# Where the slot index products of a routing group stand: four of seven groups moved by one table

## The chip, the cores and the metric

The kernel runs on one core of a Trainium2 chip. The metric is the device time of one execution in microseconds (us); before the change it is 647.14 us, the median of three runs (646.2 to 647.47). PE is the matrix engine, DVE the vector engine, ACT the scalar engine, POOL the GpSimd engine and SP the engine that issues most DMAs. PSUM is the memory that PE writes its products to and from which DVE and ACT read them.

## The reference

Attention over 8 batches, 8 heads, 576 positions and 64 numbers a head, with a causal window of 128 and a bias that falls with distance; its output, as 4608 rows ("tokens") of 512 numbers, goes into a layer of 8 experts, each token to one.

```
mask = (rel >= 0) & (rel < window)
scores = np.where(mask, scores + bias[None], -1000000000.0)
attn = np.exp(scores - max); attn = attn / (sum + 1e-09)
x = attn @ v, as (4608, 512)
logits = x @ w_gate; expert_idx = argmax(logits)
for e in range(8):
    h = np.maximum(xe @ w1[e], 0.0); ye = h @ w2[e]
    out[mask] = gate_w[mask, None] * ye
```

The tokens of an expert are gathered, computed together in tiles of 128 and scattered back. So each token needs a slot: its rank among the tokens of its expert, and each slot needs the index of its token. Finding these is the routing.

## The kernel before, in words

**Two stages.** First comes attention with the routing worked in, then the experts (`moe_static`). Attention goes over 36 chunks of 128 tokens. Its order is written out by hand, step by step: `step(s)` is called for s = 0 to 151 and records, engine by engine, what is to be done; each engine then runs its instructions in just that order. A chunk `ch` begins at step 4·ch, and the table `LAGS` says at which later steps its parts come: scores on PE (L167 the bias, L176 query times key) at steps that leave remainder 0 and 2 modulo 4, masks and row maxima on DVE (L189, L192), exponentials on ACT (L198), transposes on PE (L211) with copies on ACT (L213) and masks on POOL (L221, L223), products with v on PE (L239) at remainder 3 and some at 0, and at remainder 1 the turning back of a chunk with its gate logits on PE (L249) and the division on DVE (L254, `x_sb`).

**The PSUM tile r_ps.** L249 writes into `r_ps`, a tile of 4 quarters of 256 fp32 numbers in each of 128 partitions; of each quarter it uses the columns 0 to 143 (`XW` is 144). There is one buffer: the next chunk's L249 gets it when all readers of the last are done. The routing borrows the unused columns: `spare(st, k, n)` is quarter k of the present `r_ps`, from column 144 on. Quarter 0 serves the rank products, quarter 1 the slot index products, quarter 2 a sum in `shift_late`.

**The routing.** The chunks form groups (`GROUPS`): 0 to 4, 5 to 9, 10 to 14, 15 to 20, 21 to 26, 27 to 29, 30 to 34, and 35 by itself. When the last chunk of a group is divided, `route` is made for it, a generator in five parts:

1. expert of each token, as ones and zeros `oh` (DVE, L473 to L486, ACT L480);
2. rank products: matmuls of a triangle of ones with `oh` into quarter 0 (PE, L490, L491, L494), their use on DVE (L496 `pick`, L504 `rank`), gates (L498, L560, L562, two or more small DMAs on SP, L565) and running counts (L501, L502);
3. position in a slot tile, `lp` (DVE, L515 to L522);
4. `rr`, token numbers sorted by expert and tile (DVE, L524 to L531);
5. slot index products: two bf16 matmuls a chunk of `lp` with `rr`, summed in quarter 1 (PE, L537), and their sum onto `base` (DVE, L539).

At the end of each step the loop over `st["stages"]` runs one part of every group whose turn it is, the older group first. A group that `PACE` does not list takes a part at every step with remainder 3, from the first one after its last chunk; a group that `PACE` lists takes its parts at the steps listed. So before the change the fifth parts of the first four groups came at steps 51, 71, 91 and 115, and the second parts of the groups from chunk 5, 10, 15 and 21 at steps 59, 79, 103 and 126. `lp` and `rr` come from a pool of two buffers (`RB`). `base` is read when all groups up to chunk 26 are in it, at step 135 (`early("g")`).

```
        for k in list(st["stages"]):
            if k[1] <= s and (s in PACE[k[2]] if k[2] in PACE else s % 4 == 3):
                k[1] = s + 1
                if next(k[0], k) is k:
                    st["stages"].remove(k)
```

**Waits.** The recording layer puts in the semaphore waits itself: an instruction that writes a tile waits for earlier readers of it, one that reads it for its writer.

Of the kernel before, what the change touches and what calls it, by code (L numbers as in the profile page):

```python
# [35 lines left out]
def attention(ctx, tc, st, qT, kT, v, iw, load_c2, chunk_done, chunks, begun):  # L36
# [295 lines left out]
    def step(s):  # L332
# [11 lines left out]
# [3 lines that stand above are left out]
# [57 lines left out]
LW = (0, 0, 0, 0)  # L404
FREE_T = 146
WU = (6, 0, 0, 1, 1, 0, 0, 0, 0, 0, 0, 1, 0)
PACE = {21: (122, 126, 130, 132, 135), 27: (135, 139, 143, 146, 148), 30: (149, 150)}
GROUPS = ((0, 5), (5, 5), (10, 5), (15, 6), (21, 6), (27, 3), (30, 5), (35, 1))
EARLY = 256
LATE = 27  # L410
# [783 lines left out]
def attn_moe_kernel(ctx, tc, qT, kT, v, c2, iw, w12, out):  # L1194
# [9 lines left out]
    with ExitStack() as actx:  # L1204
# [9 lines left out]
        def done(ch, subs, x_sb):  # L1214
# [14 lines left out]
            if g == G - 1:  # L1229
# [14 lines left out]
                else:  # L1244
                    r = route(tc, st, lg, c0, G, groups)
                    st["stages"].append([r, st["step"] + (c0 not in PACE), c0])

# [46 lines left out]
```

## Time and profile before

| | before |
|---|---|
| median of 3 runs | 647.14 us |
| the profiled execution | 646.91 us, span of its instructions 645.2 us |
| granted PE clock | 0.998 |
| PE busy | 632.1 us, 98% of the span |
| DVE busy | 390.9 us, 61% |
| ACT busy | 314.1 us, 49% |
| POOL busy | 299.2 us, 46% |

The 1.7 us between the span and the time of that execution lie outside the instructions. In the profile's lines each row of a timeline gives the start in us, the duration in us, the engine, the line of the kernel, the operation, the tile written and those read, how many instructions are merged into the row, and in brackets how long the engine stood idle before it and on whom it waited. PEld is the loading of PE's weights, which runs beside its matmuls. A row of waits gives the sum in us, the number of times and the longest.

### The profile page before, as it was taken

The page shows a single profiled execution, that of the slowest core. Times are in us where ns is not written, and L with a number is a line of the kernel's source. Part 1 is how long each engine was busy: PE and PEld are TensorE (multiplying, and loading weights), DVE is VectorE, ACT ScalarE, POOL GpSimd, SP SyncE. Part 2 cuts the span into 40 slices and gives each one's busy share as a digit, 9 for nine tenths or more (in the row PEclk, how much of TensorE's full clock was granted, in tenths as well). Part 3 has the DMA queues.
Part 4 walks back from the last instruction along what each step waited for, and adds up shares of the span by engine and source line. Part 5 has one row for each costly group of instructions (what it writes and reads, how often), then busy time and mean ns, then how long its engine had stood idle before and what let it go on. Part 6 is the DMA issues. An engine that isn't in the chain of part 4 may idle for free.

```text
span 645.2 us, 15063 instructions
## 1 busy us (share of the span) xinstructions
PE 632.1 (98%) x5681; PEld 540.2 (84%) x5681; DVE 390.9 (61%) x978; ACT 314.1 (49%) x947; POOL 299.2 (46%) x414
## 2 busy tenths in 40 slices
PE   8999999999998999999999999999999999999995
PEld 4888888888887988888988898898898888888884
DVE  6578888969898785545544654555455355346411
ACT  5878889888867324433333334334233333424311
POOL 5534657769446040166236707633660660561202
PEclk9999999999999999999999999999999999999999
DMA  9958998988734263372534325333442542534101
GB/s 312 301 153 216 220 260 237 217 258 240 193 69 103 54 196 98 130 273 75 186 128 151 108 78 183 113 94 139 142 122 83 165 122 87 185 107 143 65 0 62
DMA packets 57645, 97.90 MB, mean 152 GB/s; under 512 B 11669, under 2 KB 31765, under 8 KB 56674
## 3 DMA queue, kind: packets, MB, share of 16 engines
q1 hardware_dynamic: 49090, 76.89, 39.9%
q0 software_dynamic: 8336, 19.76, 10.6%
q8 instruction: 46, 0.75, 0.5%
q10 hardware_dynamic: 144, 0.26, 0.2%
q14 instruction: 29, 0.24, 0.1%
HBM read 77.91 MB, written 18.98 MB: 150 GB/s over the span
## 4 chain that ended last, share of the span: by engine, by line
PE 67%; ACT 0%; DVE 0%; issue 0%; POOLq 0%; POOL 0%; ACTq 0%
PE y_ps L907 32%; PE l_ps L711 30%; PE s_ps L711 2%; PE x_ps L672 1%; PE b_ps L239 1%; PE y_ps L867 1%; PE r_ps L249 0%; PE x_ps L867 0%; ACT pe L198 0%; POOLq L1060 0%; PE l_ps L683 0%; DVE y L915 0%; DVE nmax L192 0%; ACT e_xh L674 0%; DVE s_ps L189 0%
## 5 line engine op out<-in xcount | busy, mean ns | idle before, releaser
L714 ACT ACTIVATE hh<-l_ps 128x336 fp32r<-128x336 f32 (+7 forms) x104 | 45.9, 446 | 203.4 <-PE l_ps L711 176.9
L718 DVE SCALAR_TENSOR_TENSOR hl<-l_ps,hh 128x336 fp32r<-128x336 f32 (+7 forms) x104 | 51.7, 501 | 152.4 <-ACT hh L714 137.5
L691 POOL DMA_INDIRECT xg<-xd,od_idx x112 | 114.8, 1025 | 35.1 <-issue 34.8
L198 ACT ACTIVATE pe<-s_ps,nmax 128x128 f32<-128x128 f32 x288 | 102.9, 382 | 33.7 <-DVE nmax L192 27.0
L907 PE MATMUL y_ps<-wh,hh 128*128 128x512 f32 (+5 forms) x280 | 111.0, 397 | 0.0
L907 PE MATMUL y_ps<-wh,hl 128*128 128x512 f32 (+5 forms) x280 | 110.4, 394 | 0.0
L907 PE MATMUL y_ps<-wl,hh 128*128 128x512 f32 (+5 forms) x280 | 110.3, 394 | 0.0
L895 POOL DMA_INDIRECT out<-y,od_pidx x33 | 34.6, 1049 | 147.8 <-ACT y L913 141.2
L999 DVE TENSOR_TENSOR wl<-w_raw,wh 128x512 fp32r<-128x512 f32 x114 | 73.9, 690 | 32.0 <-ACT wh L995 27.4
L711 PE MATMUL l_ps<-xh,wh 128*128 128x304 f32 (+9 forms) x416 | 81.8, 318 | 0.3 <-DVE hl L718 0.3
L711 PE MATMUL l_ps<-xl,wh 128*128 128x304 f32 (+9 forms) x416 | 81.1, 316 | 0.3 <-issue 0.3
L711 PE MATMUL l_ps<-xh,wl 128*128 128x304 f32 (+9 forms) x416 | 81.0, 317 | 0.0
L711 PEld LDWEIGHTS l_ps<-xh,wh 128*128 128x128 f32 x416 | 68.0, 189 | 9.0 <-issue 1.2
L711 PEld LDWEIGHTS l_ps<-xl,wh 128*128 128x128 f32 x416 | 66.3, 189 | 2.3 <-issue 0.6
L711 PEld LDWEIGHTS l_ps<-xh,wl 128*128 128x128 f32 x416 | 66.4, 189 | 1.9
L239 PE MATMUL b_ps<-pT,v_sb 128*64 128x128 f32 (+2 forms) x1136 | 65.4, 265 | 0.4 <-ACT pT L213 0.4
L239 PEld LDWEIGHTS b_ps<-pT,v_sb 128*64 128x64 f32 (+1 forms) x1136 | 56.1, 136 | 10.0 <-issue 4.9
L907 PEld LDWEIGHTS y_ps<-wh,hl 128*128 128x128 f32 (+5 forms) x280 | 51.4, 184 | 13.7 <-DVE hl L718 0.2
L907 PEld LDWEIGHTS y_ps<-wl,hh 128*128 128x128 f32 (+5 forms) x280 | 51.5, 184 | 11.3
L907 PEld LDWEIGHTS y_ps<-wh,hh 128*128 128x128 f32 (+5 forms) x280 | 51.4, 184 | 10.4 <-ACT hh L714 0.5
L995 ACT CAST wh<-w_raw 128x1024 fp32r<-128x1024 f32 x57 | 59.5, 1044 | 1.0 <-DMA w_raw<-w 1.0
L198 ACT ACTIVATION_READ_ACCUMULATOR pe<-s_ps,nmax 128x1 f32 x272 | 59.6, 219 | 0.0
(225 smaller groups left out, 958.2 us busy)
## 6 DMA issues: line engine op xcount, KB each, us to landing
w_raw<-w SPq DMA_DIRECT2D x64, 512.0 KB
q_sb<-qT SPq DMA_DIRECT2D x39, 256.0 KB
xd<-x_sb SPq DMA_DIRECT2D x32, 258.0 KB
v_sb<-v SPq DMA_DIRECT2D x32, 256.0 KB
k_sb<-kT SPq DMA_DIRECT2D x7, 1152.0 KB
w_n<-w SPq DMA_DIRECT2D x4, 1024.0 KB
xg<-xd,od_idx POOLq DMA_INDIRECT x112
xd<-x_sb SPq DMA_DIRECT2D x8, 129.0 KB
```

Source lines behind the costliest of these rows:

```text
L198: nc.scalar.activation(out=pe[:, h, :], in_=s_ps[:, c, n, lo:lo + 128], func=AF.Exp, bias=nmax[:, 2 * c + n:2 * c + n + 1], scale=1.0, **( ...
L239: nc.tensor.matmul(out=x_ps[64 * c:64 * c + 64, p, q], lhsT=blocks["v", b, m - 1 + kb][0:kk, D * h:D * h + D], rhs=pT[0:kk, kb, h, q], sta ...
L672: nc.tensor.transpose(out=x_ps[:, d, :], in_=g[:, SUB * d:SUB * d + 128], identity=st["ident"])
L691: ins = tc.nc.gpsimd.indirect_dma_start(out=g[:, s], out_offset=None, in_=parts, in_offset=bass.IndirectOffsetOnAxis(ap=idx[:, s], axis=0),)
L711: nc.tensor.matmul(out=ps, lhsT=a[:, 128 * d:128 * d + 128], rhs=b[:, d], start=(k == 0), stop=(k == 11))
L714: nc.scalar.activation(out=hh, in_=ps, func=AF.Relu)
L718: nc.vector.scalar_tensor_tensor(out=hl, in0=ps, scalar=0.0, in1=hh.bitcast(F32), op0=ALU.max, op1=ALU.subtract)
L867: nc.tensor.matmul(out=ps[m * g:m * g + n], lhsT=hrs[p][:, f, :], rhs=w2s[p][:, f % 4, w * g:w * g + w], start=f == 0, stop=f == 7)
L895: ins = nc.gpsimd.indirect_dma_start(**kw).ins
L907: nc.tensor.matmul(out=ys[t][0:n], lhsT=a[:, tl], rhs=b[:, 512:1024], start=(f == 0 and k == 0), stop=(f == 7 and k == 2))
L995: keep(tc, nc.scalar.copy(out=wh, in_=raw))
L999: keep(tc, eng.tensor_tensor(out=wl[:, sl], in0=raw[:, sl], in1=wh.bitcast(F32)[:, sl], op=ALU.subtract))
```

## The change

One table is longer: `PACE` now lists the groups that begin at chunk 0, 5, 10 and 15 too. Their first four parts stay at the steps that they had. The fifth, the slot index products and the sum onto `base`, goes from step 51 to 59, from 71 to 79, from 91 to 103 and from 115 to 126: each to the step at which the next group has its rank products, and, as the older group comes first, right ahead of them.

```
-PACE = {21: (122, 126, 130, 132, 135), 27: (135, 139, 143, 146, 148), 30: (149, 150)}
+PACE = {0: (35, 39, 43, 47, 59), 5: (55, 59, 63, 67, 79), 10: (75, 79, 83, 87, 103), 15: (99, 103, 107, 111, 126), 21: (122, 126, 130, 132, 135), 27: (135, 139, 143, 146, 148), 30: (149, 150)}
```

No instruction is added or taken away. The order on ACT, POOL and SP stays as it was; PE and DVE change at eight places, four left and four entered.

On PE, at step 51 of the old order (the products of chunks 0 to 4, ten matmuls, of which the first is shown) and the scores that follow them:

```order
 L239 MATMUL b_ps<-pT,v_sb 64x128 [waits Pool_49]
 L239 MATMUL b_ps<-pT,v_sb 64x128 x5
-L537 LDWEIGHTS lp
-L537 MATMUL r_ps<-rr,lp 128x48 [waits DVE_49]
...
-L167 LDWEIGHTS eye_sb
+L167 LDWEIGHTS eye_sb [waits DVE_49]
 L167 MATMUL s_ps<-bias_sb,eye_sb 64x2x192 [waits Activation_49]
```

The scores now follow the products with v directly. On PE at step 59 of the new order, where the ten stand ahead of the rank products of chunks 5 to 9 and in the same `r_ps` (the number behind a name tells its buffer apart; the first of the ten is shown):

```order
L239 MATMUL b_ps_1540<-pT_1404,v_sb_1353 64x128 x2
L537 LDWEIGHTS lp_1159
L537 MATMUL r_ps_1502<-rr_1256,lp_1159 128x48 [waits DVE_49]
...
L490 LDWEIGHTS tri_166
L490 MATMUL r_ps_1502<-oh_1464,tri_166 128x40 [waits DVE_49]
L491 LDWEIGHTS tri_166
```

Before, each of the two had an `r_ps` of its own. On DVE at step 126, where the sum onto `base` of chunks 15 to 20 stands between the row maxima and the first use of the rank products:

```order
 L189 COPY_PREDICATED s_ps<-mask_sb,s_ps 128x4x64
 L192 TENSOR_REDUCE nmax<-s_ps 128x4
+L539 TENSOR_TENSOR base<-base,r_ps 128x48
 L496 TENSOR_TENSOR pick<-r_ps,oh 128x48
 L498 TENSOR_REDUCE gate<-ex 128x6
```

In the built program the wait of L490 at these four places is for the count that L539 brings to DVE's semaphore; before it was for the count that L254 (`x_sb`) brings.

## The prediction

> **What bounds the kernel now.** I read the page first, then PE's waits, the stretches of the attention stage, and the timelines at the eight places. The page says which engine is full:
>
> ```profile
> PE 632.1 (98%) x5681; PEld 540.2 (84%) x5681; DVE 390.9 (61%) x978; ACT 314.1 (49%) x947; POOL 299.2 (46%) x414
> ...
> PE   8999999999998999999999999999999999999995
> ```
>
> A share over the whole run does not tell what binds where the change works, which is between 70 and 180 us. The stretches there, with PE first:
>
> ```profile
> 50.00:70.00 20.00, 20.00 (x309) 16.60 (x310) 17.04 (x48) 15.59 (x69) 9.31 (x19) 1.00 0.86 224
> ...
> 150.00:170.00 20.00, 20.00 (x318) 16.59 (x316) 18.02 (x39) 16.86 (x73) 13.80 (x22) 1.00 0.79 226
> 170.00:190.00 20.00, 19.75 (x344) 16.70 (x337) 17.67 (x53) 15.02 (x65) 11.56 (x21) 1.00 0.43 108
> ```
>
> PE is busy for 20.00 of 20 us in all six stretches from 50 to 170, while DVE and ACT, with 15 to 18, have some air, though little. All that PE waited for in the whole run:
>
> ```profile
> PE s_ps L167 <- ACT pe L198: 1.6, 3, 0.9
> PE b_ps L211 <- ACT pT L213: 1.3, 2, 0.8
> PE s_ps L119 <- DVE warm L110: 1.3, 1, 1.3
> PE r_ps L239 <- ACT pe L198: 0.7, 1, 0.7
> PE b_ps L239 <- ACT pT L213: 0.4, 1, 0.4
> PE l_ps L711 <- issue: 0.3, 1, 0.3
> PE l_ps L711 <- DVE hl L718: 0.3, 1, 0.3
> PE r_ps L537 <- DVE x_sb L254: 0.3, 1, 0.3
> ```
>
> 6.2 us in 645. So a microsecond by which PE is held up in this stage is a microsecond at the end, and one that it is spared may be one gained.
>
> **What the old places give back.** At step 51, about 70 us, the ten products and what follows them:
>
> ```profile
> 70.72 0.42 PE L537 MATMUL r_ps<-rr,lp 128*128 128x48 bf16 x10
> ...
> 71.07 0.36 PE L167 MATMUL s_ps<-bias_sb,eye_sb 64*64 64x384 bf16 x4
> ...
> 71.37 0.19 DVE L539 TENSOR_TENSOR base<-base,r_ps 128x48 f32<-128x48 f32 x1
> ...
> 160.99 0.47 PE L537 MATMUL r_ps<-rr,lp 128*128 128x48 bf16 x12
> ...
> 161.39 0.36 PE L167 MATMUL s_ps<-bias_sb,eye_sb 64*64 64x384 bf16 x4
> ```
>
> From the first of the ten to the next matmul are 71.07 - 70.72 = 0.35 us; with twelve (chunks 15 to 20) 0.40. Two more cost 0.05, so one costs 0.025, ten cost 0.25, and 0.10 of the 0.35 goes with the step from tiles of 128*128 to the 64*64 of the scores. Without the group the products with v meet the scores directly. The four places give at most 3 x 0.35 + 0.40 = 1.45 us.
>
> Not all of it comes through, because PE can only come earlier where nobody else is late. At two places somebody is:
>
> ```profile
> 101.89 0.22 ACT L198 ACTIVATION_READ_ACCUMULATOR pe<-s_ps,nmax 128x1 f32 x1
> ...
> 102.16 0.30 PE L167 MATMUL s_ps<-bias_sb,eye_sb 64*64 64x256 bf16 x4
> ...
> 160.84 0.21 ACT L198 ACTIVATION_READ_ACCUMULATOR pe<-s_ps,nmax 128x1 f32 x1
> ```
>
> The scores write over a PSUM tile that the exponentials on ACT must have read. At 102.16 PE comes 0.05 us behind the end of that reading (101.89 + 0.22 = 102.11), the handover itself; what the second place gives is caught there, and I count 0.05 of its 0.35. At 161.39 ACT had ended at 161.05, so with 0.05 of handover PE can come 0.29 earlier, not 0.40. I count 0.35 + 0.05 + 0.35 + 0.29 = 1.04.
>
> **What the new places cost: a wait.** The ten products themselves cost 0.25 again. The tile change isn't paid again, since the rank products have the same tiles. But the products write quarter 1 of `r_ps`, L539 on DVE reads it, and only then may the rank products write quarter 0 of the same buffer: their wait now asks for the count that L539 brings. PE, DVE, PE in turn, with PE idle meanwhile. Does the chip really wait where the columns are not the same? This kernel already has such a pair:
>
> ```profile
> 189.15 0.82 DVE L254 TENSOR_TENSOR x_sb<-r_ps,rinv 128x64 f32<-128x64 f32 x2
> ...
> 190.03 0.23 PE L537 MATMUL r_ps<-rr,lp 128*128 128x48 bf16 x3 [0.28 <-DVE x_sb L254]
> ```
>
> L254 reads columns 0 to 143 of the quarters, L537 writes from 144 on, no number in common, and PE stood idle for 0.28 us until L254 ended at 189.97, plus 0.06. The Trainium skill, "PSUM — Partial Sum Buffer", section "PSUM bank collisions raise a hardware error", speaks against the change in the same way: two engines may not be on one bank and the same quadrant at once, and it says to guard "by bank × quadrant (by bank is the simple version), not by address"; quarters 0 and 1 make up one bank by its 2 KiB. By that rule the wait is no accident of the recording, and the sum is the one below; if addresses decided, it would be the no-wait rival. The row above sides with the rule.
>
> The price, at step 59, where the rank products stood before at 82.10:
>
> ```profile
> 82.10 0.19 PE L490 MATMUL r_ps<-oh,tri 128*128 128x40 bf16 x1
> ...
> 82.16 0.24 PE L494 MATMUL r_ps<-oh,tri 128*128 128x32 bf16 x4
> ...
> 82.33 0.36 PE L167 MATMUL s_ps<-bias_sb,eye_sb 64*64 64x384 bf16 x4
> ...
> 82.44 0.20 DVE L496 TENSOR_TENSOR pick<-r_ps,oh 128x40 f32<-128x40 f32 x1 [1.36 <-PE r_ps L494]
> ```
>
> From the end on PE (82.40) to the reader on DVE is 0.04. So: first product at 82.10, last result at 82.52 (0.42, as at 70.72), L539 from 82.56, 0.19 long, to 82.75, handover 0.06, L490 at 82.81: 0.71 us later than before, with DVE ready all along (idle for 1.36). At step 79 it is the same, 0.71, since DVE was ready there too:
>
> ```profile
> 110.64 0.19 PE L490 MATMUL r_ps<-oh,tri 128*128 128x40 bf16 x1
> ...
> 110.98 0.20 DVE L496 TENSOR_TENSOR pick<-r_ps,oh 128x40 f32<-128x40 f32 x1 [0.60 <-PE r_ps L494]
> ```
>
> At the other two, L539 stands on DVE behind a row maximum that is not done:
>
> ```profile
> 143.92 0.20 PE L490 MATMUL r_ps<-oh,tri 128*128 128x48 bf16 x1
> ...
> 144.48 0.20 DVE L496 TENSOR_TENSOR pick<-r_ps,oh 128x48 f32<-128x48 f32 x1
> ...
> 175.96 0.20 PE L490 MATMUL r_ps<-oh,tri 128*128 128x48 bf16 x1
> ...
> 176.18 0.43 DVE L189 COPY_PREDICATED s_ps<-mask_sb,s_ps 128x256 f32<-128x256 uint32 x1 [0.44 <-PE s_ps L176]
> ...
> 176.22 1.42 PE L239 MATMUL b_ps<-pT,v_sb 128*64 128x128 f32 x22
> 176.64 0.69 DVE L192 TENSOR_REDUCE nmax<-s_ps 128x4 f32<-128x512 f32 x1
> ...
> 177.25 0.20 DVE L496 TENSOR_TENSOR pick<-r_ps,oh 128x48 f32<-128x48 f32 x1
> ```
>
> L539 takes the place of `pick`. At step 103: 144.48 + 0.19 + 0.06 = 144.73, against 143.92: 0.81. At step 126 the routing stands right behind the scores, and DVE must first mask and reduce these very scores: 177.25 + 0.19 + 0.06 = 177.50, against 175.96: 1.54. Queued behind L490 on PE there are the products with v, which before ran from 176.22 during DVE's work; they, the next scores, transposes and L249 all come later, and POOL, ACT and DVE with them.
>
> Added: 0.71 + 0.71 + 0.81 + 1.54 = 3.77. Net: 3.77 - 1.04 = 2.73; the bounds are 3.77 - 1.45 = 2.32 and, if no gain came through, 3.77.
>
> **Does it reach the end?** Behind step 126 DVE gets full, and PE waits later for it and ACT (190 to 207 us). If DVE kept its own time, these waits would swallow PE's delay. What decides is who waited for whom just after:
>
> ```profile
> 179.28 1.15 PE L249 MATMUL r_ps<-iw_sb,xT 128*128 128x144 f32 x8
> ...
> 180.47 0.82 DVE L254 TENSOR_TENSOR x_sb<-r_ps,rinv 128x64 f32<-128x64 f32 x2 [0.47 <-PE r_ps L249]
> ```
>
> DVE stood idle for 0.47 us until PE's L249 ended at 180.43. With PE 1.25 net later (1.54 - 0.29) L249 ends later by that, and DVE, which `pick` reaches only 0.6 later, still waits for it: the whole chain moves along. From 210 us on PE is the bound again.
>
> **Edits at nothing.** What L539 takes on DVE at the new places is inside the wait priced above. That its 0.19 us leave the old ones saves nothing, since DVE there stands idle for PE's next scores:
>
> ```profile
> 72.22 0.43 DVE L189 COPY_PREDICATED s_ps<-mask_sb,s_ps 128x256 f32<-128x256 uint32 x1 [0.66 <-PE s_ps L176]
> ```
>
> Were DVE full at all four, it would be 4 x 0.19 = 0.76 in the change's favour, inside the range. `lp` and `rr` are held longer, but the next group takes the other of two buffers. The moved part issues no DMA; the gate DMAs behind `pick` on SP come 0.6 to 0.8 us later, and the gathers that read them stand behind step 135. `base` is complete at step 126, read at 135. L249 waits for `pick`, which moves with PE.
>
> **The sum.** The profiled execution took 646.91 us, so 646.91 + 2.7 = 649.6; the median of the three runs lies 0.2 above it. I say 649.7. A measurement of this kernel can tell about 0.2%, 1.3 us, from no change: slower begins at 648.4.
>
> **Rivals.**
>
> - *DVE sets the pace after step 126.* For it: DVE is busy for 17.67 of 20 us there, and PE waits for others after 190. Then the 1.25 us of step 126 vanish and 1.48 stay: 648.4, right on the line. Against it: the idle 0.47 above. It decides if DVE is still busy when the late L249 ends. Chance 0.18.
> - *Every gain is caught*, by ACT as at 102.16, since PE comes earlier only if all do: 646.91 + 3.77 = 650.7. Chance 0.10.
> - *No wait where it counts: not slower.* If L539 were done before PE reached L490, or the quarters didn't hinder each other, only the tile change would go, four times 0.10: 646.5. It decides as soon as the hand to DVE and back (0.04 + 0.19 + 0.06) hides behind other matmuls; but none stand between L537 and L490. The Trainium skill, "TensorEngine Tiling (Array Packing)", "Key Properties", says that changing the tiling mode drains the engine, which bears this rival out; the 0.10 at 71.07 agrees, and it is that small. Chance 0.05.
>
> The forecast itself has 0.67, with its own range of 649.1 to 650.4.
>
> **How the numbers follow.** The range of 8 in 10 must reach the first rival (648.4) and the second (650.7); with 0.1 or 0.2 for scatter it is 648.2 to 650.8. Slower: 0.67 + 0.10 + half of 0.18, less a little for stray runs, 0.83. Same: the rest of the first rival and the third, 0.15. Faster by over 0.2%: 0.02, as not even the third rival gives 1.3 us.
>
> **What would show it.** In the profile after, PE's waits should have a new row, L490 waiting for DVE's `base`, four times, with about 0.29 at each of the first two (82.52 to 82.81), 0.39 at the third and 1.07 at the last, some 2.0 us in all, longest 1.1. L167 should follow L239 within 0.2 us at the old places, the row of 102.16 should become a wait for ACT, and the end of the attention should lie 2 to 3 us later. I am wrong if that row is missing, if L490's idle time is under 1 us in all, or if it is there and the last transposes before 207 us come no later than before.

## The result: slower by 0.6%, just above the forecast range

The changed kernel took 651.0 us (median of 6 runs, 649.8 to 651.56) beside 647.07 for the kernel before (6 runs, 646.2 to 647.47): a ratio of 1.006, with a 95% interval of 1.005 to 1.007. The direction and the four waits came as forecast; the time lies 0.2 us above the range and 1.3 above the forecast of 649.7. In the first experiment below, the same kernel took 649.85 beside 646.75, a ratio of 1.0054 (1.0041 to 1.0066).

First the list of PE's waits in the kernel after, whole. Each row gives what PE waited for, the sum in us, how often, and the longest:

```profile
PE s_ps L167 <- ACT pe L198: 2.3, 4, 0.9
PE r_ps L490 <- DVE base L539: 2.0, 4, 1.1
PE b_ps L211 <- ACT pT L213: 1.3, 2, 0.8
PE s_ps L119 <- DVE warm L110: 1.3, 1, 1.3
PE s_ps L176 <- DMA k_sb<-kT: 0.6, 1, 0.6
PE b_ps L239 <- ACT pT L213: 0.4, 1, 0.4
PE l_ps L711 <- DVE hl L718: 0.4, 1, 0.4
PE r_ps L537 <- DVE x_sb L254: 0.3, 1, 0.3
PE r_ps L239 <- DMA v_sb<-v: 0.2, 1, 0.2
```

Where the change works, two things are new against the list of before: the row of L490, four times, 2.0 us in all, as forecast; and in the row of L167 one more wait for ACT, which was not. The other differences (the two rows of DMAs, the row of L239 for L198 that is gone, those of L711) lie before 20 us or in the expert stage. The same view cut to 20 to 180 us, where the kernel before has no wait long enough to be listed, shows just these two:

```profile
PE r_ps L490 <- DVE base L539: 2.0, 4, 1.1
PE s_ps L167 <- ACT pe L198: 0.6, 1, 0.6
```

The forecast wait in the timeline of after, at step 59 and at step 126 (the idle time and its cause are in brackets):

```profile
82.14 0.20 DVE L539 TENSOR_TENSOR base<-base,r_ps 128x48 f32<-128x48 f32 x1 [1.47 <-PE r_ps L537]
82.39 0.18 PE L490 MATMUL r_ps<-oh,tri 128*128 128x40 bf16 x1 [0.29 <-DVE base L539]
...
177.89 0.47 PE L537 MATMUL r_ps<-rr,lp 128*128 128x48 bf16 x12
178.10 0.43 DVE L189 COPY_PREDICATED s_ps<-mask_sb,s_ps 128x256 f32<-128x256 uint32 x1 [0.43 <-PE s_ps L176]
178.57 0.69 DVE L192 TENSOR_REDUCE nmax<-s_ps 128x4 f32<-128x512 f32 x1
179.18 0.20 DVE L539 TENSOR_TENSOR base<-base,r_ps 128x48 f32<-128x48 f32 x1
179.43 0.18 PE L490 MATMUL r_ps<-oh,tri 128*128 128x48 bf16 x1 [1.06 <-DVE base L539]
```

At 82 us DVE had stood idle and the hand there and back is all there is to it; at 178 us the sum stands behind the mask and the row maximum of the scores, and PE waits through both.

The wait that was not forecast follows step 79, at 117 us. The rows of after:

```profile
112.98 0.18 DVE L504 TENSOR_REDUCE rank<-pick 128x5 f32<-128x40 f32 x1
113.00 1.26 POOL L1016 TENSOR_TENSOR wl<-w_raw,wh 128x512 fp32r<-128x512 f32 x1
113.20 1.09 DVE L506 TENSOR_SCALAR t<-rank 128x5 f32<-128x5 f32 x1
...
114.32 0.17 DVE L507 TENSOR_SCALAR t<-t 128x5 f32<-128x5 f32 x1
114.40 0.69 DVE L189 COPY_PREDICATED s_ps<-mask_sb,s_ps 128x512 f32<-128x512 uint32 x1
...
115.91 0.37 ACT L198 ACTIVATE pe<-s_ps,nmax 128x128 f32<-128x128 f32 x1 [1.83 <-DVE nmax L192]
...
117.47 0.36 PE L167 MATMUL s_ps<-bias_sb,eye_sb 64*64 64x384 bf16 x4 [0.62 <-ACT pe L198]
```

and those of the kernel before at the same instructions:

```profile
112.15 0.17 DVE L506 TENSOR_SCALAR t<-rank 128x5 f32<-128x5 f32 x1
112.36 0.17 DVE L507 TENSOR_SCALAR t<-t 128x5 f32<-128x5 f32 x1
...
112.70 1.27 POOL L1016 TENSOR_TENSOR wl<-w_raw,wh 128x512 fp32r<-128x512 f32 x1
...
115.78 0.36 PE L167 MATMUL s_ps<-bias_sb,eye_sb 64*64 64x384 bf16 x4
```

L506 works on five numbers a partition. In the kernel before it was over at 112.32, ahead of POOL's half subtraction L1016 (the rest of an expert's weights, for a later stage). In the kernel after, DVE is late by the wait at step 79 and POOL is not (L506 begins 1.05 us later than before, L1016 only 0.30), and L506 now begins 0.20 us into L1016; it ends at 114.29, 0.03 us after L1016 does. From there the delay runs down a chain that can be read row by row: L507, the mask L189, the row maximum, ACT idle for 1.83 us, its exponentials, and PE idle for 0.62.

To see where the time went I laid the two traces side by side at the start of each chunk's eight L249. The distance between after and before goes from 22.24 - 22.31 = -0.07 us at the first to 219.35 - 215.91 = +3.44 at the last, so the attention stage is 3.51 us longer. It changes as follows:

| place | forecast, us | measured, us |
|---|---|---|
| old place, step 51 | -0.35 | -0.35 |
| new place, step 59 | +0.71 | +0.70 |
| old place, step 71, with the next chunk | -0.05 | -0.30 + 0.31 = +0.01 |
| new place, step 79 | +0.71 | +0.70 |
| L506 under L1016, the two chunks behind | not forecast | +0.70 + 0.06 = +0.76 |
| old place, step 91, with the next chunk | -0.35 | -0.35 + 0.15 = -0.20 |
| new place, step 103 | +0.81 | +0.79 |
| old place, step 115 | -0.29 | -0.41 |
| new place, step 126 | +1.54 | +1.52 |
| sum | +2.73 | +3.52 |

### The profile page after: what moved, and what is told of

The parts are those of the page before. It is cut to its first block, busy times and chain, and to the rows that moved or that the text cites. A ratio compares the mean times of both kernels' runs of the same rounds, so it can differ in the third digit from the quotient of the medians.

```text
span 648.1 us, 15063 instructions
## 1 busy us (share of the span) xinstructions
PE 632.8 (98%) x5681; PEld 540.3 (83%) x5681; DVE 392.1 (60%) x978; ACT 314.0 (48%) x947; POOL 299.5 (46%) x414
## 4 chain that ended last, share of the span: by engine, by line
PE 66%; ACT 1%; DVE 1%; issue 0%; POOLq 0%; POOL 0%; ACTq 0%
PE y_ps L907 31%; PE l_ps L711 30%; PE s_ps L711 2%; PE x_ps L672 1%; PE b_ps L239 1%; PE y_ps L867 1%; PE r_ps L249 0%; PE x_ps L867 0%; ACT pe L198 0%; ACT wh L995 0%; POOLq L1060 0%; PE l_ps L683 0%; DVE y L915 0%; DVE wl L999 0%; DVE nmax L192 0%
## 5 line engine op out<-in xcount | busy, mean ns | idle before, releaser
L198 ACT ACTIVATE pe<-s_ps,nmax 128x128 f32<-128x128 f32 x288 | 102.8, 381 | 33.9 <-DVE nmax L192 27.5
L711 PE MATMUL l_ps<-xh,wh 128*128 128x304 f32 (+9 forms) x416 | 81.8, 318 | 0.4 <-DVE hl L718 0.4
L711 PE MATMUL l_ps<-xh,wl 128*128 128x304 f32 (+9 forms) x416 | 81.0, 316 | 0.0
L711 PE MATMUL l_ps<-xl,wh 128*128 128x304 f32 (+9 forms) x416 | 80.8, 316 | 0.0
L711 PEld LDWEIGHTS l_ps<-xh,wh 128*128 128x128 f32 x416 | 68.0, 188 | 9.2 <-issue 1.2
L711 PEld LDWEIGHTS l_ps<-xh,wl 128*128 128x128 f32 x416 | 66.3, 189 | 1.9
L711 PEld LDWEIGHTS l_ps<-xl,wh 128*128 128x128 f32 x416 | 66.3, 189 | 1.7
L239 PE MATMUL b_ps<-pT,v_sb 128*64 128x128 f32 (+2 forms) x1136 | 65.5, 265 | 0.4 <-ACT pT L213 0.4
L239 PEld LDWEIGHTS b_ps<-pT,v_sb 128*64 128x64 f32 (+1 forms) x1136 | 56.1, 136 | 10.2 <-issue 5.9
L198 ACT ACTIVATION_READ_ACCUMULATOR pe<-s_ps,nmax 128x1 f32 x272 | 59.2, 218 | 0.0
```

The source lines that it names most:

```text
L198: nc.scalar.activation(out=pe[:, h, :], in_=s_ps[:, c, n, lo:lo + 128], func=AF.Exp, bias=nmax[:, 2 * c + n:2 * c + n + 1], scale=1.0, **( ...
L239: nc.tensor.matmul(out=x_ps[64 * c:64 * c + 64, p, q], lhsT=blocks["v", b, m - 1 + kb][0:kk, D * h:D * h + D], rhs=pT[0:kk, kb, h, q], sta ...
L711: nc.tensor.matmul(out=ps, lhsT=a[:, 128 * d:128 * d + 128], rhs=b[:, d], start=(k == 0), stop=(k == 11))
```

## Experiments

Each time is shown beside that of the kernel before in the same round of runs. Beside it stands the length of the attention stage in the profiled execution, from the first chunk's first L249 to the last chunk's. It is the sharper measure: the rest of the span, in which nothing was changed, comes out differently in two executions of one kernel (648.1 - 219.35 = 428.8 us and 647.4 - 219.47 = 427.9). The experiments ran in three rounds, each on a chip of its own, but there is one trace of the kernel before, taken ahead of them all; its stage is 215.91 - 22.31 = 193.60 us.

| kernel | time, us | before, us | ratio, 95% interval | attention stage, us | longer than 193.60 by |
|---|---|---|---|---|---|
| changed kernel, the result above | 651.0 | 647.07 | 1.006 (1.005 to 1.007) | 22.24 to 219.35 | +3.51 |
| changed kernel again | 649.85 | 646.75 | 1.0054 (1.0041 to 1.0066) | 22.07 to 219.47 | +3.80 |
| POOL's pair swapped | 649.46 | 646.75 | 1.0042 (1.0030 to 1.0055) | 21.95 to 218.39 | +2.84 |
| the same, once more | 649.73 | 647.15 | 1.0037 (1.0024 to 1.0051) | 22.33 to 218.76 | +2.83 |
| sum behind the rank products | 648.11 | 646.75 | 1.0025 (1.0017 to 1.0034) | 22.48 to 217.53 | +1.45 |
| both | 647.2 | 646.5 | 1.0014 (1.0005 to 1.0023) | 22.50 to 216.82 | +0.72 |
| only the last group moved | 647.91 | 646.5 | 1.0016 (1.0007 to 1.0025) | 21.97 to 217.11 | +1.54 |
| only the first three moved | 649.36 | 646.5 | 1.0039 (1.0025 to 1.0053) | 22.35 to 218.63 | +2.68 |
| put off, no partner | 647.1 | 646.5 | 1.0016 (1.0007 to 1.0025) | 22.52 to 216.72 | +0.60 |
| before, with POOL's pair swapped | 647.69 | 647.15 | 1.0006 (0.9997 to 1.0015) | 22.24 to 216.19 | +0.35 |

**The changed kernel again.** No edit.

> The changed kernel once more, nothing edited, for a second profile and more times. Its first profiled execution was 649.8 us, 1.2 under its median of 651.0. If the waits for the sum onto base and the slow L506 at 113.20 are of the kernel and not of that one execution, both stand in the new profile too: L490 waiting for DVE 4 times, 2.0 us in all, L506 1.09 us long, L167 waiting 0.6 us for ACT at about 117. Time 650 to 651.5. If the slow L506 was chance, that wait is missing and the attention ends 0.7 us earlier.

Both stand in the new profile. PE's waits from 20 to 180 us:

```profile
PE r_ps L490 <- DVE base L539: 2.0, 4, 1.1
PE s_ps L167 <- ACT pe L198: 0.7, 1, 0.7
```

and the pair on DVE and POOL, with what PE makes of it:

```profile
112.88 1.27 POOL L1016 TENSOR_TENSOR wl<-w_raw,wh 128x512 fp32r<-128x512 f32 x1
112.99 1.20 DVE L506 TENSOR_SCALAR t<-rank 128x5 f32<-128x5 f32 x1
...
117.37 0.36 PE L167 MATMUL s_ps<-bias_sb,eye_sb 64*64 64x384 bf16 x4 [0.68 <-ACT pe L198]
```

L506 ends at 114.19, 0.04 us after L1016 again. The slow L506 belongs to the kernel, not to one execution. The time fell just under what I had expected. The stage is 0.29 longer than in the first execution of the same program, and 0.18 of that is one more meeting of DVE and POOL, which comes and goes. In this execution and, below, in the first one:

```profile
189.88 0.67 POOL L223 TENSOR_SCALAR_AFFINE_SELECT pT<-pT 128x512 f32<-128x512 f32 x1
189.90 0.66 DVE L524 TENSOR_TENSOR c<-c,t 128x6 f32<-128x6 f32 x1
...
189.95 0.69 POOL L223 TENSOR_SCALAR_AFFINE_SELECT pT<-pT 128x512 f32<-128x512 f32 x1
189.95 0.16 DVE L524 TENSOR_TENSOR c<-c,t 128x6 f32<-128x6 f32 x1
```

Where L524 is long, PE's L537 behind it waits 0.45 us for `x_sb`, elsewhere 0.27 to 0.29. L524 is long here, in both runs with POOL's pair swapped, in "both", in "only the last group" and in "only the first three", and each of these six stages is 0.17 or 0.18 us longer by it; the others, that of before too, are not. Two executions of one program differ in it, so it is not the change's.

**POOL's pair swapped.** The one half subtraction that L506 meets is recorded two steps earlier (step 78, not 80), which moves it ahead of its neighbour L182 on POOL and changes nothing else on any engine:

```
-        n, i = divmod(s - FETCH, 8)
+        n, i = (-1, 0) if s == 80 else (2, 7) if s == 78 else divmod(s - FETCH, 8)
```

> Two neighbours on POOL change places: the second half subtraction L1016 that stood at 113.00 goes ahead of the small sum L182, into POOL's idle time from 111.0 to 112.8; nothing else changes. Theory (DVE and POOL hinder each other): L506 goes back from 1.09 to about 0.17 us, the wait of PE's L167 for ACT at 117.47 (0.62) goes, the chunk begun there is 0.7 us earlier, and the time is 0.7 under the changed kernel, 650.3. Rival (L506 is long for another reason, or the wait is what DVE's lateness of 0.7 from step 79 brings anyway): L506 may shorten, but PE's wait stays and the time is 651.0.

The timeline of this kernel at the same place:

```profile
110.71 1.27 POOL L1016 TENSOR_TENSOR wl<-w_raw,wh 128x512 fp32r<-128x512 f32 x1
...
111.37 0.18 PE L490 MATMUL r_ps<-oh,tri 128*128 128x40 bf16 x1 [0.30 <-DVE base L539]
...
112.92 0.17 DVE L506 TENSOR_SCALAR t<-rank 128x5 f32<-128x5 f32 x1
...
114.72 0.37 ACT L198 ACTIVATE pe<-s_ps,nmax 128x128 f32<-128x128 f32 x1 [0.91 <-DVE nmax L192]
...
116.50 0.36 PE L167 MATMUL s_ps<-bias_sb,eye_sb 64*64 64x384 bf16 x4
```

L506 is back at 0.17, ACT waits for half as long, and PE reaches L167 with no wait at all, though the wait of L490 just ahead is as before. Between 20 and 180 us the row of L490, four times and 2.0 us in all, is the only one left in the list of PE's waits.

The stage is 0.96 us shorter than in the changed kernel run beside it (196.44 against 197.40): 0.81 in the two chunks behind L506, and 0.15 because what step 91 gives no longer goes back in part. By the trace the theory stands and the rival falls. In the time itself only 0.4 of that shows (649.46 against 649.85, intervals that overlap), so it was run once more.

> The changed kernel with the swap on POOL once more, for more times beside those of the kernel before. Theory: the attention ends 2.8 us later than before, not 3.5 to 3.8 as without the swap; time 2.6 to 3.0 over the kernel before. Rival (the swap brings nothing that reaches the end): 3.1 to 3.9 over it.

The stage is +2.83 again (+2.66 without the long L524), the time by the medians 2.58 us over the kernel before: just under what the theory gave, and below the rival's. The interval of the ratio (1.6 to 3.3 us) reaches into both, so it is the traces that decide.

**The swap by itself.** The same line in the kernel before, as a control.

> The kernel before, with the two neighbours on POOL in the other order, as a control. Theory (the swap is worth something only where L506 or L507 lies under L1016, and in the kernel before they end at 112.53, ahead of its start at 112.70): no change, within 0.3 us of the kernel before, L507 and L506 at 0.17, at most L560 some 0.3 longer. Rival (the swap is good in itself): 0.7 to 1.0 us under the kernel before.

Not faster: 1.0006, an interval that holds 1. So the swap is worth something only where it undoes a meeting. It even makes another one here, since L1016 now lies at 110.67 to 111.93, and on DVE stands:

```profile
111.28 0.68 DVE L560 TENSOR_SCALAR gate<-gate 128x5 f32<-128x5 f32 x1
...
112.63 0.17 DVE L506 TENSOR_SCALAR t<-rank 128x5 f32<-128x5 f32 x1
112.83 0.17 DVE L507 TENSOR_SCALAR t<-t 128x5 f32<-128x5 f32 x1
```

L560 took 0.17 in the kernel before; here it ends at 111.96, 0.03 after L1016, and the stage is 0.35 longer, 0.25 + 0.07 of it in the two chunks behind. I had expected 0.3 more of L560 and got 0.5.

**The sum behind the rank products.** The products stay at the new places; only L539 goes behind L496 on DVE:

```
-    nc.vector.tensor_tensor(out=st["base"], in0=st["base"], in1=ip, op=ALU.add)
+    st["owed"] = lambda: nc.vector.tensor_tensor(out=st["base"], in0=st["base"], in1=ip, op=ALU.add); c0 < 21 or st.pop("owed")()
...
-    nc.vector.tensor_tensor(out=pick, ..., in1=oh, op=ALU.mult)
+    nc.vector.tensor_tensor(out=pick, ..., in1=oh, op=ALU.mult); st.pop("owed", lambda: None)()
```

> The four index products stay at their new places, but the sum onto base (L539) is issued on DVE behind the use of the rank products (L496), so that the rank products follow the index products on PE with no DVE between them. Theory (the hand to DVE and back is the cost): L490 waits for DVE no more, each new place costs 0.25 us of matmuls in place of 0.71 to 1.54, 4 x 0.25 = 1.0 against 1.04 given back: the time is that of the kernel before, 646.5 to 647.3, or up to 0.7 more if DVE's L506 or L507 meets POOL's L1016 here as well. Rival (the place is bad in itself: later index products, longer held lp and rr, a fuller DVE): 649 or more.

The timeline of this kernel at step 59: the rank products follow the ten on PE's heels, and so do the scores.

```profile
81.92 0.42 PE L537 MATMUL r_ps<-rr,lp 128*128 128x48 bf16 x10
82.19 0.18 PE L490 MATMUL r_ps<-oh,tri 128*128 128x40 bf16 x1
...
82.41 0.36 PE L167 MATMUL s_ps<-bias_sb,eye_sb 64*64 64x384 bf16 x4
```

The new places now cost 0.25, 0.25, 0.25 and 0.30 us. That the time is still 1.4 over the kernel before, a little more than I had allowed, is the meeting once more, this time of the next instruction:

```profile
112.80 1.27 POOL L1016 TENSOR_TENSOR wl<-w_raw,wh 128x512 fp32r<-128x512 f32 x1
112.81 1.29 DVE L507 TENSOR_SCALAR t<-t 128x5 f32<-128x5 f32 x1
...
117.08 0.36 PE L167 MATMUL s_ps<-bias_sb,eye_sb 64*64 64x384 bf16 x4 [0.88 <-ACT pe L198]
```

DVE reaches L507 0.45 us later than in the kernel before (112.81 against 112.36), enough to be caught by 0.01 us, for 0.95 + 0.07 of delay at the two chunks behind.

**Both.**

> Both mends together: the sum onto base behind the use of the rank products, and the half subtraction on POOL ahead of the small sum. Theory (the hand to DVE and back, and DVE's L507 under POOL's L1016, are the whole loss): of the 1.5 us that the attention of the kernel with the sum behind ends late (1.67 at the experts' first product, less 0.18 at its first chunk), the 0.95 at the slow L507 go, some 0.5 stay (four times 0.25 of matmuls, given back only in part where ACT is late): 0.4 to 0.6 over the kernel before, no wait for ACT at 117. Rival (something else in the put-off products costs): still 1 us or more over the kernel before.

0.7 us over the kernel before, and neither wait is left between 20 and 180 us. L507 takes 0.17 again. The stage is 0.73 shorter than with the sum alone put behind. It is 0.72 longer than before, of which 0.17 is the long L524; the other 0.55 is what I had expected. The four old places gave 0.35 + 0.30 + 0.35 + 0.24, the new ones took 1.05, 0.67 of the gains went back in the chunks behind (0.31, 0.16 + 0.12, 0.08), and 0.07 more came in the second chunk behind step 79. L560, begun 0.29 us before the end of L1016, took 0.31 there; whether the 0.07 come of it is not shown. The loss is thus explained by the two causes, but for what the matmuls cost at their new places and the gains that go back.

**Only the last group, only the first three.** `PACE` gets the entry of 15 alone, or those of 0, 5 and 10 alone.

> Only the group from chunk 15 is put off (115 to 126), the other three stay. Theory (each place has its own price): -0.41 at the old place, +1.52 at step 126, with one wait of L490 for DVE, 1.06 us: 1.1 us over the kernel before. Rival (DVE, full behind step 126, sets the pace once PE is not late already): the wait is there but under 0.5 us of it reach the end.

> Only the first three groups are put off (to 59, 79, 103), the last stays. Theory: -0.35 + 0.70 + 0.01 + 0.70 + 0.75 (slow L506) - 0.20 + 0.79 = 2.5 us over the kernel before by the end of the attention, of which 0.75 are the collision of DVE and POOL; L490 waits 3 times, 0.97 us in all. Rival (the slow L506 came of something that group 15 does, or is chance): 1.7.

With the last alone L490 waits once, for 1.06 us, and step 126 costs 1.51. The old place gave less than in the changed kernel, 0.26, of which 0.07 went back; with 0.18 of the long L524 and 0.04 elsewhere the stage is 1.54 longer, more than the expected 1.1; the time (1.4 by the medians, 0.5 to 1.6 by the interval) doesn't tell the two apart. The wait reaches the end in full, so DVE does not set the pace there. With the first three alone the list for 20 to 180 us reads

```profile
PE r_ps L490 <- DVE base L539: 1.0, 3, 0.4
PE s_ps L167 <- ACT pe L198: 0.7, 1, 0.7
```

and the stage is 2.68 longer, 0.75 of it from 112.30 to 117.21 in the time of before, where L506 takes 1.19, and 0.18 at the long L524; without that it is the 2.5 of the theory. So the meeting needs nothing of the last group; the lateness by step 79 is enough.

**Put off, with no partner.** The fifth parts go to steps 55, 75, 95 and 119, one chunk later than before, where no rank products follow.

> All four products are put off, but by one step of remainder 3 only (to 55, 75, 95 and 119), where no rank products follow. Theory (the partner costs, not the putting off): the ten or twelve matmuls and their tile change are paid in one place instead of the other, no wait of L490 for DVE, time within 0.5 us of the kernel before. Rival (products later, lp and rr held longer, cost of themselves): 1 us or more over it.

No wait of PE between 20 and 180 us, and none of L490; 647.1 beside 646.5 by the medians, 0.5 to 1.6 by the interval of the ratio, and a stage 0.60 longer. By the medians this is just outside the theory's 0.5, and short of the rival's 1 us; the interval allows both. So putting the products off is not quite free (the old places give 0.35, 0.29, 0.35 and 0.27, of which 0.31 goes back behind step 71, and the new ones cost 0.36, 0.36, 0.36 and 0.48), but it is a small part of the 3.5 to 3.8. The 0.36 beside the 0.25 of the kernel with the sum behind, where the rank products follow, also bear out the 0.10 that the prediction gave the step between tiles. No version beat the kernel before: none of the places tried for these products is better.

## Why the prediction was right, and where it was wrong

**Right: the wait and its price.** L490 waits four times for the sum onto `base`, 0.29, 0.30, 0.38 and 1.06 us, and the four new places cost 0.70, 0.70, 0.79 and 1.52 against the 0.71, 0.71, 0.81 and 1.54 that were worked out. Taking away DVE's part alone (the sum behind) leaves 0.25 to 0.30 a place. The rule of the Trainium skill that the prediction cited on banks is not tested by this: the wait stands in the program, because both products are in one buffer, and the chip only obeyed. Nor does the row at 190.03 side with that rule, as the prediction has it: there too both instructions use one `r_ps`, and the wait is the program's. Whether the chip would need it wasn't tried.

**Right, within 0.15 us: what the old places give.** Step 51 gave 0.35, step 71 nothing after ACT had caught it, step 91 0.20 for 0.35 and step 115 0.41 for 0.29; 0.95 in all against 1.04. That the sum is so near is in part luck, since the last two are off in opposite directions. The row of 102.16 did turn into one behind ACT: in after L167 starts at 102.46 and the exponentials had ended at 102.40. At step 115 ACT caught nothing in the changed kernel, in which PE was already late: the exponentials had ended at 162.93, L167 came at 163.32. With only the last group moved they ended at 160.76, L167 came at 160.81, and the place gave 0.26, near the 0.29.

**Right: it reaches the end.** The 3.45 us by which the chunk behind step 126 is late (182.73 against 179.28) are 3.44 at the last one. DVE did not set the pace. The end of the attention lies 3.5 us later, not the 2 to 3 named as a sign, and that is the next point.

**Wrong: a term was missing.** The step that failed is in "Edits at nothing". It said that what L539 takes on DVE is inside the wait, followed DVE's lateness through L496 to the gates and no further, and so put at nothing what late small instructions on DVE meet on POOL. L496 is followed by eight more small instructions, the last of which stood 0.17 us ahead of a POOL instruction of 1.27 us (112.53 to 112.70) that doesn't move with them, since L182, ahead of it on POOL, waits for ACT. A shift of 0.7 pushed L506 under it: by the rows of before alone, 112.15 + 0.71 = 112.86 is 0.16 us inside L1016. The price in the changed kernel is 0.76 us of stage by the offsets; by the swap it is 0.96 against the second execution and, with the long L524 taken out, 0.85 against the first. The sum without it, 2.73, is within 0.1 of the stage of the two runs with the swap (+2.66 each without the long L524) and within 0.2 of their times (+2.71 and +2.58). So the other terms of the sum were right in size together, and the range was too low at the top: its upper end, 650.7 for "every gain is caught", took in no meeting that the kernel before doesn't have.

The Trainium skill, "SBUF — State Buffer", section "Who interferes with whom", states a rule that would have pointed to it: VectorE and GpSimd share one pair of SBUF ports, and when a VectorE instruction needs that pair too, whoever issues first holds it for its whole instruction and "the other fully blocks"; `tensor_scalar` can be such an instruction, `tensor_reduce` on trn2 cannot. The traces here agree: L506, L507 and L560, all TENSOR_SCALAR, ended 0.03 to 0.04 us after L1016 whenever they began within it, and a TENSOR_REDUCE keeps its 0.20 under a mask on POOL. The trace of before holds such a meeting at its full price, 8 us ahead of L506 and with another L1016: L477, on 128x40 numbers, takes 1.22 us, where at 139.94, with nothing on POOL, it takes 0.21. And L484, 0.18 to 0.21 us with POOL idle, lasts until the mask is done (105.83):

```profile
103.97 1.27 POOL L1016 TENSOR_TENSOR wl<-w_raw,wh 128x512 fp32r<-128x512 f32 x1
104.08 1.22 DVE L477 SCALAR_TENSOR_TENSOR key<-sh,c_sb 128x40 f32<-128x40 f32 x1
105.19 0.64 POOL L221 TENSOR_SCALAR_AFFINE_SELECT pT<-pT 128x512 f32<-128x512 f32 x1
105.33 0.20 DVE L482 TENSOR_REDUCE mk<-key 128x5 f32<-128x40 f32 x1
...
105.56 0.32 DVE L484 TENSOR_TENSOR oh<-key,mk 128x40 bf16<-128x40 f32 x1
```

**What is left open.** In the first result the median is 3.9 us above that of before, in the first experiment 3.1, and the stage gives 3.5 and 3.8; between the profiled executions of before and of the first result it is 649.80 - 646.91 = 2.89, near the forecast 2.73 only because the expert stage, which no edit touches, came out shorter there. The meeting thus explains 0.8 to 1.0 of the 1.3 us by which the median lies above the forecast; what the rest is stays open. The rest of the run scatters by more than half a microsecond on its own, and I can't say which share of the 1.2 us between the profiled execution of after and its median is of that kind.

## What to carry to other kernels

When a change makes an engine late, follow it past the first reader, through all the small instructions that come with it, and look at what stands on the engine beside it: one that doesn't move with it can turn 0.17 us into 1.1. A trace taken before the change shows such meetings too: an instruction that is long in one group and short in the next, with a row of the other engine over it. Two products in one PSUM buffer with a reader between them cost, where the program waits by buffer as here, a trip to the reading engine and back; put the reader behind both, and they cost only their matmuls. Lay the two traces side by side at a row that comes once per chunk, and a sum of many terms can be tested term by term.

## What the runs showed that was not expected

A DVE instruction of 0.17 us on 128x5 numbers took 1.09, 1.20, 1.19, 1.29, 0.68 and 0.31 us when it began within a POOL instruction of 1.26 to 1.28, and each ended with it; 0.01 us decided in one case (112.81 against 112.80). At L524 two executions of one program differ for as little: 0.16 us or 0.66.

The expert stage, in which no kernel here differs, has stops that come and go. In the profiled execution of before:

```profile
286.26 0.41 PE L711 MATMUL l_ps<-xl,wh 128*128 128x336 f32 x1 [0.31 <-issue]
```

In both executions of the changed kernel this stop is missing, and the offset against before falls by 0.58 us there. What causes it is open.
